# Letting the first two FFN blocks start on half a block of tokens, in a fused top-k attention and SwiGLU kernel

## The chip, the cores and the metric

The kernel runs on one core of one Trainium2 chip. The metric is device time in microseconds of one execution. A core has a TensorE (PE, with its weight loads listed apart as PEld), a VectorE (DVE), a ScalarE (ACT), a GpSimd (POOL) and DMA queues. Each engine works through its own instructions in the order in which the program emitted them and waits for the others by semaphores, so where in the program a piece of work is emitted decides what stands behind it.

## What is computed

```python
# attention: batch 8, heads 8, seq 576, head_dim 64, float32
scores = scale * np.matmul(q, k.transpose(0, 1, 3, 2))
kth = np.partition(scores, -32, axis=-1)[..., -32:-31]
scores = np.where(scores >= kth, scores, -1e9)
attn = softmax(scores)                       # abridged
attn_out = np.matmul(attn, v)
# bridge: (B,H,S,D) -> x of (4608 tokens, 512)
g = x @ w_gate                               # 512 -> 1536
silu = g * (1.0 / (1.0 + np.exp(-g)))
val = x @ w_val                              # 512 -> 1536
out = silu * val @ w_out                     # 1536 -> 512
```

## The kernel before

**Units and turns.** Attention is cut into 160 units, in the order batch, query tile, head pair. A batch has four query tiles of 128 tokens and a fifth of 64, each with four head pairs; a unit of a full tile handles two heads side by side, one of the fifth tile handles its two heads of 64 rows in one go, so it is half a unit of VectorE work. The main loop makes one *turn* for each unit. In turn `n`, VectorE selects the 32 largest scores of unit `n`; ScalarE and GpSimd weigh unit `n-1`; TensorE transposes the weights of unit `n-3`, multiplies those of unit `n-4` by the values, and computes the scores of unit `n+1`.

**FFN pieces.** What attention leaves goes to `xT`, in 18 blocks of 256 tokens. When a block has all its tokens from all head pairs (`done`), its FFN is fed to TensorE in *pieces*: 24 pieces of gate and value products (four matmuls of 256 columns each) and 12 pieces of the output product. A turn adds 4.6 (a half unit's turn 2.3) to a credit that is capped at 8, and a piece costs 1.

**Rounding of the weights.** The three weight matrices arrive in 72 pieces of 128 x 256, and each goes through ScalarE, GpSimd and VectorE before it may be used. This is spread over the turns: in five of every eleven VectorE steps a `rounding(1)` is made, which emits one stage of each of several pieces.

```python
    def weights():
        # ... 48 pieces of w_gate and w_val in turns, then 24 of w_out
        lags = (5, 3, 2, 0)
        for n in range(len(pieces) + lags[0]):
            for lag in lags:
                if 0 <= n - lag < len(pieces):
                    next(pieces[n - lag], None)
            ready[0] = max(n - lags[0] + 1, 0)
            yield

    def rounded(src, dst):                      # four stages, cut
        nc.sync.dma_start(w[:], ...);                                   yield
        nc.scalar.activation(size[:], high.bitcast(FP32), AF.Abs)       # L101
        nc.gpsimd.tensor_scalar(size[:], size[:], HUGE, LEAST, ...)     # L103
        nc.scalar.mul(ulps[:], low.bitcast(U32), 2.0**-29);             yield   # L106
        nc.vector.tensor_scalar(bits, bits, 3, 0x3FFFFFFF, ...)         # L110
        nc.gpsimd.tensor_tensor(bits, bits, ulps[:], ALU.add);          yield   # L113
        nc.vector.scalar_tensor_tensor(out=dst.bitcast(I32), ...)       # L116

    def need(n):
        while ready[0] < n:
            next(weight)
# ...
    def feed(kb):                               # the FFN of one block
        x = xT.pop(kb)
        hs = []
        def product(w, s, then):
            ps = ps_f.tile([P, 2, BLK], FP32, tag="f", name="f")
            need(8 * s + (4 if w is wg else 8))
            for i in range(2):
                m = 2 * s + i
                for kc in range(KC):            # 4
                    nc.tensor.matmul(ps[:, i, :], w[:, kc, m * P : (m + 1) * P],
                                     x[:, kc, :], ...)                  # L412
                if i == 1:
                    on_act.append(lambda: then(ps))
                yield
        for s in range(MS):                     # 6
            h = ffn.tile([P, 2, BLK], FP32, tag="h", name="h", bufs=MS + 1)
            hs.append(h)
            def gate(ps, h=h):
                nc.scalar.activation(h[:], ps[:], AF.Tanh, scale=0.5)   # L430
                nc.scalar.mul(half[:], ps[:], 0.5)                      # L431
                nc.scalar.add(h[:], h[:], 1.0)                          # L432
                on_pool.append(lambda: nc.gpsimd.tensor_mul(h[:], h[:], half[:]))  # L433
            def value(ps, h=h):
                nc.scalar.copy(val[:], ps[:])                           # L437
                on_pool.append(lambda: nc.gpsimd.tensor_mul(h[:], h[:], val[:]))   # L438
            yield from product(wg, s, gate)
            yield from product(wv, s, value)
        for t in range(BLK // P):
            for m in range(MC):                 # 12
                need(8 * MS + 2 * m + 2)
                nc.tensor.matmul(ps[:], hs[m // 2][:, m % 2, t * P : (t + 1) * P],
                                 wo[:, m, :], ...)                      # L449
                # ... evacuation and store after the last
                if m % 2 == 1:
                    yield

    def piece():
        # ... flush what waits for ScalarE and GpSimd, if there is more than one
        while True:
            if not current:
                if not todo or done.get(todo[0], 0) < NHP * BLK:
                    return False
                current.append(feed(todo.pop(0)))
            if next(current[0], 0) == 0:
                current.pop()
                continue
            return True
    def pieces(n):
        for _ in range(n):
            if credit[0] >= 1 and piece():
                credit[0] -= 1
# ...
    for n in range(NU + VALUES):                # one turn
        if n >= NU - NHP: credit[0] = 8.0
        else: credit[0] = min(credit[0] + (4.6 if nh == 2 else 2.3), 8.0)
        flush(on_act)
        # ... penalize(n-1): POOL e L293
        flush(on_pool)
        # ... turn(n-3): PE etps L329; finish_unit(n-4): PE av L349, L358
        # ... scores(n+1): PE s L250; weigh(n-1): ACT e L302; ACT sc L255
        dve(2, beside=False)
        pieces(2)
        flush(on_act); flush(on_pool)
        dve(1); dve(1)
        # ... normalize(n-2), part of prep
        pieces(1); dve(1); pieces(1); dve(2)
        run(topk)                               # ends with DVE e L281
        pieces(6)
    while piece():
        pass
```

Of the kernel before, what the change touches and what calls it, by code (L numbers as in the profile page):

```python
# [8 lines left out]
AF = mybir.ActivationFunctionType  # L9
ALU = mybir.AluOpType  # L10
FP32 = mybir.dt.float32
# [4 lines left out]
P = 128  # L16
# [4 lines left out]
BLK = 256  # L21
# [6 lines left out]
def kernel(  # L28
# [27 lines left out]
    nc = tc.nc  # L56
# [5 lines left out]
    NHP = H // 2  # L62
    KC = DM // P
    MC = DFF // P
    MS = MC // 2
    NBLK = B * S // BLK
    scale = 1.0 / float(D) ** 0.5
# [8 lines left out]
    ffn = ctx.enter_context(tc.tile_pool(name="ffn", bufs=2))  # L76
# [11 lines left out]
    wg = consts.tile([P, KC, DFF], FP32, name="wg")  # L88
    wv = consts.tile([P, KC, DFF], FP32, name="wv")
# [31 lines left out]
    def weights():  # L121

        pieces = []
        for f in range(0, DFF, WP):
            for src, dst in ((w_gate, wg), (w_val, wv)):
                for c in range(KC):
                    pieces.append((src[c * P : (c + 1) * P, f : f + WP], dst[:, c, f : f + WP]))
        for c in range(MC):
            for f in range(0, DM, WP):
                pieces.append((w_out[c * P : (c + 1) * P, f : f + WP], wo[:, c, f : f + WP]))  # L130
        pieces = [rounded(*p) for p in pieces]
# [8 lines that stand above are left out]
    ready = [0]  # L140
    weight = weights()
# [2 lines left out]
        for _ in range(n):  # L144
            next(weight, None)

    def need(n):

        while ready[0] < n:
            next(weight)  # L150

    pairs = [(b, hp) for b in range(B) for hp in range(NHP)]
    raw, preps = {}, {}
# [184 lines left out]
    xT, done = {}, {}  # L338
# [41 lines left out]
    def store(o, g0):  # L380

        at = g0
        while at < g0 + P:
            b, c = divmod(at, S)
            j, p0 = divmod(c, P)
            n = min(g0 + P - at, S - c, P - p0)
            r0 = b * S + (c if j == J else J * p0 + j)
            dst = out[r0 : r0 + n, :] if j == J else out[r0 : r0 + J * (n - 1) + 1 : J, :]
            nc.sync.dma_start(dst, o[at - g0 : at - g0 + n, :])
            at += n  # L390

    on_act, on_pool = [], []

    def flush(queue):
        while queue:
            queue.pop(0)()

    def feed(kb):

        x = xT.pop(kb)
        hs = []

        def product(w, s, then):
            ps = ps_f.tile([P, 2, BLK], FP32, tag="f", name="f")
            need(8 * s + (4 if w is wg else 8))
            for i in range(2):
                m = 2 * s + i  # L410
                for kc in range(KC):
                    nc.tensor.matmul(  # L412
                        ps[:, i, :],
                        w[:, kc, m * P : (m + 1) * P],
                        x[:, kc, :],
                        start=(kc == 0),
                        stop=(kc == KC - 1),
                    )
                if i == 1:
                    on_act.append(lambda: then(ps))  # L420
                yield

        for s in range(MS):
            h = ffn.tile([P, 2, BLK], FP32, tag="h", name="h", bufs=MS + 1)
            hs.append(h)


            def gate(ps, h=h):
                half = ffn.tile([P, 2, BLK], FP32, tag="gv", name="half_g", bufs=3)
                nc.scalar.activation(h[:], ps[:], AF.Tanh, scale=0.5)  # L430
                nc.scalar.mul(half[:], ps[:], 0.5)  # L431
                nc.scalar.add(h[:], h[:], 1.0)  # L432
                on_pool.append(lambda: nc.gpsimd.tensor_mul(h[:], h[:], half[:]))  # L433

            def value(ps, h=h):
                val = ffn.tile([P, 2, BLK], FP32, tag="gv", name="val", bufs=3)
                nc.scalar.copy(val[:], ps[:])  # L437
                on_pool.append(lambda: nc.gpsimd.tensor_mul(h[:], h[:], val[:]))  # L438

            yield from product(wg, s, gate)  # L440
            yield from product(wv, s, value)
        for t in range(BLK // P):
            ps = ps_f.tile([P, DM], FP32, tag="f", name="o_ps")
            for m in range(MC):
                need(8 * MS + 2 * m + 2)
                if m == 6:
                    flush(on_act)
                    flush(on_pool)
                nc.tensor.matmul(  # L449
                    ps[:],  # L450
                    hs[m // 2][:, m % 2, t * P : (t + 1) * P],
                    wo[:, m, :],
                    start=(m == 0),
                    stop=(m == MC - 1),
                )
                if m == MC - 1:

                    def finish(ps=ps, t=t):
                        o = ffn.tile([P, DM], FP32, tag="o", name="o")
                        nc.scalar.copy(o[:], ps[:])  # L460
                        store(o, kb * BLK + t * P)

                    on_act.append(finish)
                if m % 2 == 1:
                    yield

    NU = len(units)
    todo = list(range(NBLK))
    current = []

    def piece():

        if len(on_act) > 1:
            flush(on_act)
        if len(on_pool) > 1:
            flush(on_pool)
        while True:
            if not current:
                if not todo or done.get(todo[0], 0) < NHP * BLK:
                    return False  # L480
                flush(on_act)
                flush(on_pool)
                current.append(feed(todo.pop(0)))
            if next(current[0], 0) == 0:
                current.pop()
                continue
            return True

    def fetch(n):

# [5 lines left out]
            load(i + NHP)  # L496

    def pieces(n):
        for _ in range(n):
            if credit[0] >= 1 and piece():  # L500
                credit[0] -= 1

    def run(steps):
        for _ in steps:
# [14 lines left out]
    credit = [0.0]  # L519
# [4 lines left out]
    for n in range(NU + VALUES):  # L524
# [37 lines left out]
        if n < NHP:  # L562
            load_v(n)
# [3 lines that stand above are left out]
# [12 lines left out]
    while piece():  # L579
        pass  # L580
# [48 lines left out]
```

## Time and profile before

| What | Value |
|---|---|
| time, median of three runs | 1914.77 us (1911.7 to 1914.82) |
| span of the profiled execution | 1913.4 us |
| busy: PE, DVE, ACT, POOL | 1756.5, 1608.9, 1156.3, 816.0 us |
| gate and value matmuls (L412), records of 256 columns | 3456, in 1728 of each weight |
| output matmuls (L449), records of 512 columns | 864 |
| first gate product starts at | 167.1 us |
| last selection on VectorE ends at | about 1820 us |

Shares of busy time are averages over stages with different limits, so the span is best cut at the turns. The last VectorE instruction of a turn's selection is `e L281`, so its starts date the ends of the turns. A float32 matmul of this kernel appears in the trace as two MATMUL records, each with a weight load of its own, while a transpose appears as one. The duration of a MATMUL record contains the time in the pipeline; what a row of matmuls takes is seen from the distance of their starts. In the timeline a group of like instructions is one row: start, length from the first start to the last end, engine, line, shapes and number.

### The profile page before, as it was taken

What the parts mean: (1) busy time and instruction counts of PE and PEld (TensorE: products, weight loads), DVE (VectorE), ACT (ScalarE), POOL (GpSimd) and SP (SyncE); (2) the same over time, 40 slices, a digit from 0 to 9 for tenths busy, and PEclk for the clock granted to TensorE, in tenths of its full rate; (3) what the DMA queues carried; (4) which work ended last, traced back from release to release, by engine and by line L of the source; (5) the groups of instructions that cost most, each with busy time, mean ns of one, the idle gap of its engine ahead of it and who ended that gap; (6) DMA issues with size and microseconds to landing.
All of it is one profiled execution on the core that took longest, in us unless ns stands there. A gap on an engine that the chain in (4) does not pass through costs nothing.

```text
span 1913.4 us, 29363 instructions
## 1 busy us (share of the span) xinstructions
PE 1756.5 (92%) x10144; PEld 1297.0 (68%) x10144; DVE 1608.9 (84%) x3476; ACT 1156.3 (60%) x2821; POOL 816.0 (43%) x846
## 2 busy tenths in 40 slices
PE   3437789989999999999999999999999999999999
PEld 2336558667677777676768676868686868586866
DVE  7999889998899979998799979999799989999400
ACT  5656656566666656675657566656675656665421
POOL 4566644335343525353335343525243535353412
PEclk7668899989999999999999999999999999999999
DMA  7322202000300012000210003000210001000000
GB/s 185 88 78 82 67 22 69 11 1 3 76 12 12 2 27 63 12 1 13 53 37 1 12 4 87 1 12 1 60 31 12 1 14 45 18 1 12 1 12 11
DMA packets 111253, 59.58 MB, mean 31 GB/s; under 512 B 89088, under 2 KB 97280, under 8 KB 111104
## 3 DMA queue, kind: packets, MB, share of 16 engines
q1 hardware_dynamic: 109904, 57.41, 11.5%
q8 instruction: 80, 1.31, 0.3%
q14 instruction: 69, 0.57, 0.1%
q10 hardware_dynamic: 1200, 0.30, 0.1%
HBM read 48.23 MB, written 9.44 MB: 30 GB/s over the span
## 4 chain that ended last, share of the span: by engine, by line
PE 82%; DVE 6%; POOL 5%; ACT 4%; issue 2%; DMA 0%; SPq 0%; POOLq 0%; DVEq 0%; ACTq 0%
PE f L412 38%; PE o_ps L449 19%; PE av L358 8%; PE etps L329 7%; PE s L250 7%; DVE m L271 2%; POOL e L293 2%; DVE rest L275 2%; PE s L236 2%; ACT e L302 1%; PE av L349 1%; PE kqps L205 1%; ACT sc L255 1%; POOL size L113 1%; POOL size L103 1%
## 5 line engine op out<-in xcount | busy, mean ns | idle before, releaser
L271 DVE MAX8 m<-rest 128x8 f32<-128x576 f32 x864 | 615.2, 747 | 2.2
L275 DVE MATCH_REPLACE8 rest<-m,rest 128x576 f32<-128x576 f32 x576 | 424.1, 743 | 0.0
L412 PE MATMUL f<-xT,wg 128*128 128x256 f32 x1728 | 407.5, 386 | 0.0
L293 POOL TENSOR_TENSOR e<-e,sc 128x1152 f32<-128x1152 f32 (+1 forms) x160 | 382.7, 2392 | 42.4 <-DVE e L281 38.8
L412 PE MATMUL f<-xT,wv 128*128 128x256 f32 x1728 | 395.8, 381 | 0.0
L449 PE MATMUL o_ps<-wo,h 128*128 128x512 f32 x864 | 387.6, 598 | 0.0
L412 PEld LDWEIGHTS f<-xT,wg 128*128 128x128 f32 x1728 | 324.2, 191 | 71.5 <-issue 29.9
L412 PEld LDWEIGHTS f<-xT,wv 128*128 128x128 f32 x1728 | 325.3, 190 | 53.3 <-issue 10.5
L433 POOL TENSOR_TENSOR h<-h,half_g 128x512 f32<-128x512 f32 x108 | 138.4, 1282 | 453.0 <-ACT h L432 435.0
L271 DVE MAX8 m<-sc 128x8 f32<-128x576 f32 x288 | 205.6, 750 | 123.9 <-ACT sc L255 78.8
L329 PE MATMUL etps<-ident,e 128*128 128x128 f32 (+1 forms) x1312 | 187.5, 288 | 125.9 <-POOL size L103 48.1
L449 PEld LDWEIGHTS o_ps<-wo,h 128*128 128x128 f32 x864 | 159.4, 190 | 193.1 <-issue 186.9
L329 PEld LDWEIGHTS etps<-ident,e 128*128 128x128 f32 (+1 forms) x1312 | 159.4, 147 | 176.1 <-POOL size L103 51.3
L330 ACT COPY et<-etps 128x512 f32<-128x512 f32 (+1 forms) x448 | 184.7, 482 | 148.5 <-PE etps L329 147.1
L302 ACT ACTIVATE e<-e,bias 128x576 f32<-128x576 f32 x288 | 222.1, 776 | 74.9 <-POOL e L293 74.5
L317 ACT ACTIVATE e<-e,tot 128x576 f32<-128x576 f32 x288 | 210.5, 780 | 5.4 <-DVE tot L314 5.1
L275 DVE MATCH_REPLACE8 rest<-m,sc 128x576 f32<-128x576 f32 x288 | 211.9, 742 | 0.0
L438 POOL TENSOR_TENSOR h<-h,val 128x512 f32<-128x512 f32 x108 | 139.7, 1293 | 149.6 <-ACT val L437 149.6
L250 PE MATMUL s<-kqT 64*128 64x288 f32 x1024 | 173.1, 446 | 9.6 <-ACT kqT L210 6.4
L312 POOL TENSOR_SCALAR tot<-tot 128x2 f32<-128x2 f32 (+1 forms) x160 | 37.4, 234 | 329.3 <-ACT e L302 320.9
L358 PE MATMUL av<-et,v 128*64 128x128 f32 (+1 forms) x2560 | 174.6, 282 | 0.0
L255 ACT COPY sc<-s 128x288 f32<-128x288 f32 x512 | 165.0, 410 | 2.5 <-PE s L250 2.5
(44 smaller groups left out, 1436.0 us busy)
## 6 DMA issues: line engine op xcount, KB each, us to landing
kq_in<-in_k_dram SPq DMA_DIRECT2D x64, 128.0 KB, 2.8
v<-in_v_dram SPq DMA_DIRECT2D x32, 256.0 KB, 3.0
kq_in<-in_q_dram SPq DMA_DIRECT2D x62, 128.0 KB, 3.1
w<-in_moe_w_gate_dram SPq DMA_DIRECT2D x24, 256.0 KB, 2.7
w<-in_moe_w_val_dram SPq DMA_DIRECT2D x24, 256.0 KB, 2.7
w<-in_moe_w_out_dram SPq DMA_DIRECT2D x24, 256.0 KB, 2.6
out_dram<-o SPq DMA_DIRECT2D x40, 128.0 KB, 2.4
out_dram<-o SPq DMA_DIRECT2D x16, 256.0 KB, 2.3
```

Of the source, the lines that this page charges most:

```text
L250: nc.tensor.matmul(ps[:, 0:half], slab[d, q0 : q0 + P], slab[d, k0 : k0 + half])
L255: nc.scalar.copy(sc[:, i * half : (i + 1) * half], ps[:, 0:half])
L271: nc.vector.max(m[:, t, 8 * r : 8 * r + 8], cur[:, hs])
L275: nc.vector.match_replace(rest[:, hs], m[:, t, 8 * r : 8 * r + 8], cur[:, hs], LOWEST)
L293: nc.gpsimd.tensor_tensor(e[:, every], e[:, every], sc[:, every], ALU.add)
L302: nc.scalar.activation(e[:, hs], e[:, hs], AF.Exp, bias=bias[:, t : t + 1], scale=scale, accum_out=tot[:, t : t + 1],)
L317: nc.scalar.mul(e[:, hs], e[:, hs], tot[:, t : t + 1])
L329: nc.tensor.transpose(ps[0:kl, c * P : (c + 1) * P], e[:, k0 : k0 + kl], ident[:])
L330: nc.scalar.copy(et[0:kl, c0 : c0 + cn, :], ps[0:kl, 0 : cn * P].rearrange("p (c j) -> p c j", c=cn),)
L358: nc.tensor.matmul(av[hh * R : (hh + 1) * R, 0:ql], v_last[:, hh, :] if c == J else vt[:, hh, c, :], moving, start=last and c == 0, stop=c ...
L412: nc.tensor.matmul(ps[:, i, :], w[:, kc, m * P : (m + 1) * P], x[:, kc, :], start=(kc == 0), stop=(kc == KC - 1),)
L449: nc.tensor.matmul(ps[:], hs[m // 2][:, m % 2, t * P : (t + 1) * P], wo[:, m, :], start=(m == 0), stop=(m == MC - 1),)
```

## The change

The gate and value products of blocks 0 and 1 are made in two halves of 128 columns. A half may start when its own 128 tokens are there, which for block 0 is four units earlier than the whole block. Where the weights for a product aren't rounded yet, the FFN no longer forces the rounding (`need`), but gives up its place in this turn (`until` yields 0) and tries again at the next. A piece of a half costs half a credit. The output product and the other 16 blocks stay as they were, and so does everything in attention.

```diff
-    def need(n):
+    def until(n):
         while ready[0] < n:
-            next(weight)
+            yield 0
...
+    def parts(kb):
+        return [slice(0, P), slice(P, BLK)] if kb < 2 else [slice(0, BLK)]
...
-        def product(w, s, then):
+        def product(w, s, c, then):
+            n = c.stop - c.start
+            yield from until(8 * s + (4 if w is wg else 8))
             ps = ps_f.tile([P, 2, BLK], FP32, tag="f", name="f")
-            need(8 * s + (4 if w is wg else 8))
             for i in range(2):
                 m = 2 * s + i
                 for kc in range(KC):
                     nc.tensor.matmul(
-                        ps[:, i, :],
+                        ps[:, i, 0:n],
                         w[:, kc, m * P : (m + 1) * P],
-                        x[:, kc, :],
+                        x[:, kc, c],
...
-                    on_act.append(lambda: then(ps))
-                yield
+                    on_act.append(lambda: then(ps[:, :, 0:n], c))
+                yield n / BLK
...
+        for c in parts(kb):
+            while done[kb] < NHP * c.stop:
+                yield 0
+            for s in range(MS):
+                if c.start == 0:
+                    hs.append(ffn.tile([P, 2, BLK], FP32, tag="h", name="h", bufs=MS + 1))
+                h = hs[s]
...             # gate and value as before, on the columns c of h, half_g and val
...
-                need(8 * MS + 2 * m + 2)
+                yield from until(8 * MS + 2 * m + 2)
...
                 if m % 2 == 1:
-                    yield
+                    yield 1
...
-                if not todo or done.get(todo[0], 0) < NHP * BLK:
-                    return False
+                if not todo or done.get(todo[0], 0) < NHP * parts(todo[0])[0].stop:
+                    return 0
...
     def pieces(n):
-        for _ in range(n):
-            if credit[0] >= 1 and piece():
-                credit[0] -= 1
+        while n > 0 and credit[0] >= 1:
+            size = piece()
+            if not size:
+                break
+            n -= size
+            credit[0] -= size
```

More of the change, by code (lines that the diff above doesn't have):

```diff
@@ L396, in flush @@
             queue.pop(0)()
+    def parts(kb):
+        return [slice(0, P), slice(P, BLK)] if kb < 2 else [slice(0, BLK)]
     def feed(kb):
-        x = xT.pop(kb)
+        x = xT[kb]
         hs = []
-        def product(w, s, then):
+        def product(w, s, c, then):
+            n = c.stop - c.start
+            yield from until(8 * s + (4 if w is wg else 8))
             ps = ps_f.tile([P, 2, BLK], FP32, tag="f", name="f")
-            need(8 * s + (4 if w is wg else 8))
             for i in range(2):
@@ L419, in product, with gate, value @@
                 if i == 1:
-                    on_act.append(lambda: then(ps))
-                yield
[L423 to L441, printed above, removed]
+                    on_act.append(lambda: then(ps[:, :, 0:n], c))
[7 more added lines that the diff above has]
+                h = hs[s]
+                def gate(ps, c, h=h):
+                    half = ffn.tile([P, 2, BLK], FP32, tag="gv", name="half_g", bufs=3)
+                    hc, gc = h[:, :, c], half[:, :, c]
+                    nc.scalar.activation(hc, ps, AF.Tanh, scale=0.5)
+                    nc.scalar.mul(gc, ps, 0.5)
+                    nc.scalar.add(hc, hc, 1.0)
+                    on_pool.append(lambda: nc.gpsimd.tensor_mul(hc, hc, gc))
+                def value(ps, c, h=h):
+                    val = ffn.tile([P, 2, BLK], FP32, tag="gv", name="val", bufs=3)
+                    hc, vc = h[:, :, c], val[:, :, c]
+                    nc.scalar.copy(vc, ps)
+                    on_pool.append(lambda: nc.gpsimd.tensor_mul(hc, hc, vc))
+                yield from product(wg, s, c, gate)
+                yield from product(wv, s, c, value)
+        del xT[kb]
         for t in range(BLK // P):
@@ L483, in piece @@
                 current.append(feed(todo.pop(0)))
[L484 to L487, printed above, removed]
+            size = next(current[0], None)
+            if size is not None:
+                return size
+            current.pop()
     def fetch(n):
```

## The prediction, made before the changed kernel was run

> **What bounds the kernel now.** I read first the busy shares in 40 slices of the span, then the sums by stage, then the dates of the turns.
>
> ```profile
> PE   3437789989999999999999999999999999999999
> ...
> DVE  7999889998899979998799979999799989999400
> ...
> PEclk7668899989999999999999999999999999999999
> ```
>
> TensorE is idle for a good half of the first three slices (of 47.8 us) and full from the eighth on. The change aims at this hole. I cut the span where the FFN starts (turn 11), where the rounding of the weights ends (turn 15), and where block 1 is finished (turn 27). In the view of windows each row has the stretch, its length, and the busy time of PE, PEld, DVE, ACT and POOL, then the granted clock:
>
> ```profile
> 110.00:166.00 56.00, 23.18 (x142) 18.76 (x141) 52.95 (x130) 35.02 (x93) 33.25 (x49) 0.63 0.29 86
> 166.00:253.00 87.00, 74.38 (x383) 57.18 (x383) 71.95 (x160) 54.28 (x134) 55.23 (x71) 0.92 0.18 56
> 253.00:372.00 119.00, 114.34 (x676) 81.20 (x675) 109.97 (x234) 74.28 (x184) 48.77 (x49) 0.99 0.15 38
> 372.00:405.00 33.00, 24.85 (x143) 16.90 (x143) 31.51 (x70) 20.53 (x52) 9.33 (x10) 0.83 0.02 9
> 405.00:1800.00 1395.00, 1371.37 (x8105) 1018.45 (x8102) 1239.19 (x2642) 877.65 (x2128) 586.46 (x555) 1.00 0.09 21
> ```
>
> To 166 VectorE is the bound (53 of 56). From 166 to 253 no engine is (PE 74, DVE 72 of 87). From 253 to 372 it is TensorE (114 of 119), with VectorE close. From 372 to 405 TensorE waits again: block 2 has no tokens yet. After 405 TensorE is the bound to the end.
>
> The dates of the turns, from the timeline of VectorE (the last operation of a selection, for turns 6, 10, 15, 25, 27 and 30; two records in a full turn, one in a half):
>
> ```profile
> 108.89 1.18 DVE L281 TENSOR_SCALAR e<-sc,m 128x576 f32<-128x576 f32 x2
> ...
> 165.71 1.42 DVE L281 TENSOR_SCALAR e<-sc,m 128x576 f32<-128x576 f32 x2
> ...
> 252.41 0.93 DVE L281 TENSOR_SCALAR e<-sc,m 128x576 f32<-128x576 f32 x2
> ...
> 346.56 1.19 DVE L281 TENSOR_SCALAR e<-sc,m 128x576 f32<-128x576 f32 x2
> ...
> 371.16 0.93 DVE L281 TENSOR_SCALAR e<-sc,m 128x576 f32<-128x576 f32 x2
> ...
> 404.43 0.94 DVE L281 TENSOR_SCALAR e<-sc,m 128x576 f32<-128x576 f32 x2
> ```
>
> A turn with rounding and no FFN takes 56.8 / 4 = 14.2 us (turns 7 to 10). One with both takes 86.7 / 5 = 17.34 us (turns 11 to 15), so the FFN adds 3.1 us to each, 15.7 in all, though neither PE nor DVE is full. Why is seen on VectorE in turn 12:
>
> ```profile
> 192.52 0.41 DVE L116 SCALAR_TENSOR_TENSOR wo<-w,size 128x256 int32<-128x256 int32 x1
> 195.81 0.29 DVE L110 TENSOR_SCALAR size<-size 128x256 int32<-128x256 int32 x1 [2.88 <-POOL size L103]
> ```
>
> VectorE waits 2.88 us for a rounding step on GpSimd (L103), which stands behind the step on ScalarE (L101), and that one behind the three gate operations of the FFN, made from 191.64 to 193.12; on GpSimd the gate's multiply of 1.27 us (L433) lies between as well.
>
> **What the Trainium skill says.** The page "TensorE: Matmul & The Clock Gate", section "Back-to-back issue gap", gives N / 2.4 ns plus 2.5 between matmuls of N columns, so half the columns take half the time; its section "LDWEIGHTS (loading the stationary operand)" puts a load at columns / 1.2, which is 107 ns for 128. The trace of before has both: nine transposes, each a load of 128 columns and a matmul of 128, go by in 0.98 us (602.43 to 603.41), 109 ns each; eight gate records of 256 columns take 1.73 us, 216 ns each. A half record should thus cost 109 ns, with its load just hidden. The same page, section "What's actually happening", has the clock at half after an idle window of about 3.4 us; the trace agrees, as the nine transposes take 1.95 us after each idle gap of 8 us. "VectorE: DVE Perf Modes", section "The TRN2 errata — SBUF-src ops pay a fixed extra latency per instruction", says that small ScalarE operations don't shrink with their size. The trace agrees: 512 columns take 597 ns, 256 take 444 (L430, L101).
>
> **The change part by part.** The order of emission doesn't depend on time, so I followed credit, `done` and `ready` turn by turn through the program's own rules. Before: no product ever finds its weights unrounded, so `need` forces nothing. FFN credits spent in turns 11 to 27 are 8, 4, 5, 4, 5 (two of them output) | 2, 2, 3, 2 | 5, 4, 5, 4, 5, 5, 4, 5: 72 for two blocks. None is spent in turns 28 to 30, and the credit stands at 8 when block 2 comes in turn 31.
>
> After, in turns 7 to 27: 7.5, 1.5, 2, 1 | 7.5, 4.5, 3, 1, 1 | 7.5, 2, 2.5, 2 | 4.5, 5, 4.5, 5, 4, 5, 1, 0: again 72. The first half of block 0 runs in turns 7 to 10, held back by the rounding from turn 8 on. The second runs in turns 11 and 12, since its tokens come at turn 11 as before; the output product then crawls in turns 13 to 15, as `wo` isn't rounded. Its remaining seven pieces come in a heap in turn 16, a half turn, followed at once by block 1.
>
> In turn 31 both programs are in the same state, and from there they emit the same instructions in the same order. TensorE is idle in turns 28 to 30 in both, so nothing carries over: the whole effect is by how much turn 30 ends earlier or later than 404.4. The 12 credits that move ahead of turn 11 fill idle TensorE time, but shorten the path only where TensorE is the bound.
>
> *Turns 7 to 15.* Bare: 9 x 14.2 = 127.8 us, before 143.5 with 15.7 of surcharge. The surcharge comes from ScalarE and GpSimd operations that stand ahead of the rounding. For a gate of 512 columns these are 1.48 + 1.27 = 2.75 us; of 256, three starts 0.33 us apart (the distance of L101 and L106 at 256 columns) and a multiply of 0.74 (L113): 1.73, so 63%. There are 24 halves in place of 12 wholes: 15.7 x 2 x 0.63 = 19.8. I take off 2 for turns 9 and 10, whose few products fit into slack. So 18, or **+2 us**.
>
> *Turns 16 to 27.* Turn 16 gets 7.5 credits where it had 2. A credit is 1.73 us, so 9.5 us more on TensorE; of this 3.3 fall into the idle time before turn 17's transposes (259.12), some 3 more into idle time and a cold clock of turns 17 and 18 that the heap removes, and 0.9 are given back in turn 18 (2.5 for 3). That leaves about 2 us of lateness. Turns 19 to 25 have 30 credits in both, so it stays. Turns 26 and 27 lose 8 credits, but VectorE has 10.56 us in each (its pace in turn 28), and before they took 24.6: the most to be had is 3.5, and most of it isn't, as their lateness is that of scores made behind turn 25's pieces, which stay. A cold TensorE at turn 16, after three nearly empty turns, costs another 1. So **+2 us**, if the matmuls of halves run at 109 ns.
>
> Sum: +4, less 1 for a warmer TensorE in turns 8 to 16, so 1914.8 + 3 = 1918.
>
> **The rivals.** (a) *The hole gets filled:* the FFN of half a block vanishes into idle time and the surcharge isn't paid in turns 7 to 10, because TensorE was idle 60% there. Then the surcharge is only that of the 12 half products in turns 11 and 12 (10 us for 15.7), and turns 26 and 27 give their 3.5: about 1906. For it speaks the idle TensorE, against it that VectorE was busy 53 of 56 us there and that the rounding waits for ScalarE and GpSimd, not for TensorE. The floor, with no surcharge at all (-15.7) and turns 16 to 27 at VectorE's pace (8 x 10.56 + 4 x 5.28 = 105.6 us for 118.8, so -13), is 1886. (b) *Loads bind the halves:* a gate load has a record of 190 ns where a transpose's has 148; if a half record took 150 ns in place of 109, block 1's 384 half records, in turns where TensorE is the bound, would cost 384 x 0.041 = 16 us: 1934. Against it: the loads of av (L358, 64 columns, no transposes) follow each other at 64 ns (16 from 615.96 to 616.98), about 128 for 128 columns. (c) *Heaps:* 7.5 credits (13 us) in turn 7 hold up ScalarE, then the rounding in turn 8, more than I took; with the heap in turn 16 this could make 10 us more: 1928.
>
> **Range and chances.** I predict 1918 us. Rival (a) sets the low end at 1906, (b) and (c) the high end at 1930. A change of 2% is 38 us, more than the floor of (a) gains and about what (b) and (c) at their worst cost together. Faster by over 2%: 0.01; within: 0.97; slower: 0.02.
>
> **What would show it.** The first gate product starts near 109 us (turn 7) rather than 167. Turn 15 ends near 254, where it ended at 252.4; earlier than 247 speaks for (a). Half records start 109 ns apart; 150 would be (b). In turns 8 and 12 VectorE waits for L103 as before. Turn 16's TensorE work is some 17 us long and turn 17 starts late. From turn 31 on all rows are the same, shifted by one number. I am wrong if that later part changes by itself, or if turns 7 to 10 keep their 14.2 us with the FFN in them.

## The result, and the profile after

The changed kernel takes 1921.74 us (median of 6 runs, 1921.6 to 1922.17) against 1914.12 us before (6 runs, 1911.7 to 1914.82). The ratio is 1.0042, 95% interval 1.0029 to 1.0055: 7.6 us slower, inside the range and within 2%, on the side that was forecast and some 4 us beyond the 1918 that was.

The busy shares in 40 slices of the changed kernel:

```profile
PE   3466789869999999999899999999999999999999
...
DVE  7988889998899979998799979999799989999400
...
PEclk7688899989999999999999999999999999999989
```

TensorE has its first FFN work in the third slice (at 109.8 us) where before it came in the fourth (167.1). The third slice rises from 3 to 6 tenths for it, and the fourth, eighth and ninth fall by 1, 1 and 2: work has moved forward, and the span hasn't got shorter. The dates of the turns in the timeline of VectorE (ends of turns 6, 10, 15, 19, 25 and 30):

```profile
108.36 1.18 DVE L281 TENSOR_SCALAR e<-sc,m 128x576 f32<-128x576 f32 x2
...
175.51 1.42 DVE L281 TENSOR_SCALAR e<-sc,m 128x576 f32<-128x576 f32 x2
...
254.04 0.94 DVE L281 TENSOR_SCALAR e<-sc,m 128x576 f32<-128x576 f32 x2
...
288.63 0.52 DVE L281 TENSOR_SCALAR e<-sc,m 128x576 f32<-128x576 f32 x1
...
358.00 0.94 DVE L281 TENSOR_SCALAR e<-sc,m 128x576 f32<-128x576 f32 x2
...
412.31 0.95 DVE L281 TENSOR_SCALAR e<-sc,m 128x576 f32<-128x576 f32 x2
```

Differences of such dates are the yardstick for all that follows. Turns 7 to 15 take 145.7 us (143.5 before), turns 16 to 19 34.6 (27.3), turns 20 to 25 69.4 (66.9), turns 26 to 30 54.3 (57.9). So +2.2, +7.3, +2.5 and -3.6: turn 30 ends 8 us later than before. What follows it is the same program in both. Busy times in the stretches between those dates, from the view of windows of the changed kernel (stretch, length, PE, PEld, DVE, ACT, POOL, then the granted clock):

```profile
108.40:175.50 67.10, 44.19 (x308) 38.05 (x305) 58.02 (x131) 41.72 (x114) 42.19 (x61) 0.83 0.24 74
175.50:254.00 78.50, 58.03 (x395) 43.36 (x395) 68.35 (x159) 49.32 (x133) 51.88 (x73) 0.87 0.20 62
254.00:288.60 34.60, 34.08 (x238) 24.48 (x238) 25.22 (x51) 18.93 (x49) 11.03 (x14) 0.98 0.07 21
288.60:358.00 69.40, 68.67 (x580) 56.77 (x577) 64.04 (x137) 46.27 (x134) 32.12 (x39) 1.00 0.23 56
358.00:412.30 54.30, 34.28 (x215) 23.72 (x215) 52.86 (x116) 33.16 (x83) 16.18 (x17) 0.87 0.02 6
```

The third row is where most of the time went: in turns 16 to 19 TensorE is busy for 34.1 of 34.6 us and VectorE for 25.2. The last row is where some came back: VectorE is busy 52.9 of 54.3.

What happens there starts with the heap of turn 16. On VectorE, the end of turn 17 and the first operation of turn 18:

```profile
267.58 0.52 DVE L281 TENSOR_SCALAR e<-sc,m 128x576 f32<-128x576 f32 x1
274.41 0.76 DVE L271 MAX8 m<-sc 128x8 f32<-128x576 f32 x1 [6.31 <-ACT sc L241]
```

Turns 16 and 17 still run on scores made earlier (7.3 and 6.25 us); turn 18 waits 6.31 us for its scores to be copied by ScalarE (L241). ScalarE in the same time:

```profile
269.56 0.58 ACT L472 COPY o<-o_ps 128x512 f32<-128x512 f32 x1 [7.75 <-PE o_ps L461]
270.88 1.24 ACT L330 COPY et<-etps 128x512 f32<-128x512 f32 x3 [0.74 <-PE etps L329]
...
273.62 0.69 ACT L241 COPY sc<-s 128x288 f32<-128x288 f32 x2
```

And TensorE:

```profile
258.09 11.43 PE L461 MATMUL o_ps<-wo,h 128*128 128x512 f32 x26 [0.23 <-DVE wo L116]
269.36 1.05 PE L417 MATMUL f<-xT,wg 128*128 128x128 f32 x8
270.25 1.15 PE L329 MATMUL etps<-ident,e 128*128 128x128 f32 x9
...
272.57 1.19 PE L236 MATMUL s<-kqT 64*64 64x288 f32 x8
```

TensorE makes the heap of output records for 11.4 us. The scores of unit 18 stand behind it and start at 272.57. ScalarE's 7.75 us of idle time before the copy of the block's output are an effect of the heap and not what holds up the scores: TensorE works without a gap from 258.09 to 277.53, and ScalarE is idle again (0.74 us) before the next copies. In the kernel before, the same scores started 9.9 us earlier:

```profile
262.64 1.81 PE L236 MATMUL s<-kqT 64*64 64x288 f32 x8
```

VectorE didn't wait for them there. A half turn has only 6.25 us of VectorE work to cover a delay, so in the changed kernel VectorE waits 6.31 us.

### The profile page after: what moved, and what is told of

Same layout as the page of the kernel before. It is cut to its first block, busy times and chain, and to the rows that moved or that the text cites. A ratio compares the mean times of both kernels' runs of the same rounds, so it can differ in the third digit from the quotient of the medians.

```text
span 1920.2 us, 30215 instructions
## 1 busy us (share of the span) xinstructions
PE 1757.8 (92%) x10528; PEld 1308.7 (68%) x10528; DVE 1611.0 (84%) x3476; ACT 1159.8 (60%) x2869; POOL 820.1 (43%) x870
## 3 DMA queue, kind: packets, MB, share of 16 engines
q8 instruction: 83, 1.36, 0.3%
## 4 chain that ended last, share of the span: by engine, by line
PE 80%; DVE 7%; POOL 5%; ACT 4%; issue 3%; DMA 0%; SPq 0%; POOLq 0%; DVEq 0%; ACTq 0%
PE f L417 38%; PE o_ps L461 18%; PE av L358 7%; PE etps L329 7%; PE s L250 6%; DVE m L271 3%; DVE rest L275 3%; POOL e L293 2%; PE s L236 2%; PE av L349 1%; ACT e L302 1%; PE kqps L205 1%; ACT sc L255 1%; POOL size L113 1%; POOL size L103 1%
## 5 line engine op out<-in xcount | busy, mean ns | idle before, releaser
L417 PE MATMUL f<-xT,wv 128*128 128x256 f32 (+1 forms) x1920 | 406.0, 363 | 17.5 <-DVE wv L116 9.5
L417 PE MATMUL f<-xT,wg 128*128 128x256 f32 (+1 forms) x1920 | 411.8, 365 | 4.5 <-DVE wg L116 4.5
L461 PE MATMUL o_ps<-wo,h 128*128 128x512 f32 x864 | 392.9, 604 | 16.5 <-DVE wo L116 16.5
L293 POOL TENSOR_TENSOR e<-e,sc 128x1152 f32<-128x1152 f32 (+1 forms) x160 | 382.9, 2393 | 49.0 <-DVE e L281 33.4
L417 PEld LDWEIGHTS f<-xT,wv 128*128 128x128 f32 x1920 | 338.2, 193 | 69.9 <-issue 12.2
L417 PEld LDWEIGHTS f<-xT,wg 128*128 128x128 f32 x1920 | 335.0, 192 | 70.3 <-issue 28.1
L443 POOL TENSOR_TENSOR h<-h,half_g 128x512 f32<-128x512 f32 (+1 forms) x120 | 141.6, 1180 | 450.5 <-ACT h L442 433.7
L329 PEld LDWEIGHTS etps<-ident,e 128*128 128x128 f32 (+1 forms) x1312 | 159.9, 147 | 143.9 <-issue 66.9
L449 POOL TENSOR_TENSOR h<-h,val 128x512 f32<-128x512 f32 (+1 forms) x120 | 141.4, 1178 | 164.5 <-ACT val L448 164.0
L250 PE MATMUL s<-kqT 64*128 64x288 f32 x1024 | 168.9, 440 | 9.0 <-ACT kqT L210 5.8
L358 PE MATMUL av<-et,v 128*64 128x128 f32 (+1 forms) x2560 | 168.5, 276 | 0.0
L440 ACT ACTIVATE h<-f 128x512 f32<-128x512 f32 (+1 forms) x120 | 66.8, 557 | 165.0 <-PE f L417 163.6
```

Source lines behind the costliest of these rows:

```text
L250: nc.tensor.matmul(ps[:, 0:half], slab[d, q0 : q0 + P], slab[d, k0 : k0 + half])
L293: nc.gpsimd.tensor_tensor(e[:, every], e[:, every], sc[:, every], ALU.add)
L329: nc.tensor.transpose(ps[0:kl, c * P : (c + 1) * P], e[:, k0 : k0 + kl], ident[:])
L358: nc.tensor.matmul(av[hh * R : (hh + 1) * R, 0:ql], v_last[:, hh, :] if c == J else vt[:, hh, c, :], moving, start=last and c == 0, stop=c ...
L417: nc.tensor.matmul(ps[:, i, 0:n], w[:, kc, m * P : (m + 1) * P], x[:, kc, c], start=(kc == 0), stop=(kc == KC - 1),)
L443: on_pool.append(lambda: nc.gpsimd.tensor_mul(hc, hc, gc))
```

## The experiments

Each is compared with the kernel before, run beside it on the same chip. The ratio is worked out from all executions of both, not from the medians. The table gives the turns' times in us from the timeline of VectorE, one profiled execution each; "t7-15" is from the end of turn 6 to the end of turn 15. The profiled execution of e1_late took 4.7 us more than the median of its kernel, that of e4_even_before 3.5 us less; the others lie within 1 us.

| Kernel | t7-15 | t16-19 | t20-25 | t26-30 | median, us | ratio (interval) |
|---|---|---|---|---|---|---|
| before | 143.5 | 27.3 | 66.9 | 57.9 | 1914.1 | |
| the change | 145.7 | 34.6 | 69.4 | 54.3 | 1921.7 | 1.0042 (1.0029, 1.0055) |
| e1_late | 147.5 | 28.1 | 70.1 | 55.8 | 1917.6 | 1.0027 (1.0017, 1.0038) |
| e2_spread16 | 146.0 | 26.0 | 68.8 | 55.8 | 1914.5 | 1.0010 (1.0001, 1.0018) |
| e3_even_after | 146.4 | 26.0 | 63.0 | 52.8 | 1907.8 | 0.9968 (0.9957, 0.9980) |
| e4_even_before | 142.4 | 28.6 | 64.5 | 52.8 | 1910.9 | 0.9984 (0.9977, 0.9992) |
| e5_lag_before | 133.9 | 27.4 | 66.9 | 57.9 | 1900.3 | 0.9928 (0.9914, 0.9941) |
| e6_lag_even_after | 135.7 | 26.3 | 64.0 | 52.8 | 1892.5 | 0.9886 (0.9873, 0.9900) |
| e7_forced | 153.9 | 28.2 | 67.6 | 53.6 | 1923.4 | 1.0048 (1.0034, 1.0061) |
| e8_lag_even_before | 130.9 | 29.3 | 64.5 | 52.8 | 1895.7 | 0.9905 (0.9892, 0.9919) |
| e9_lag_after | 137.0 | 36.5 | 69.4 | 54.3 | 1912.0 | 0.9989 (0.9983, 0.9996) |
| e10_even_before_31 | 130.7 | 29.3 | 64.5 | 52.8 | 1894.0 | 0.9897 (0.9880, 0.9913) |
| e11_even_after_again | 135.7 | 26.3 | 64.0 | 52.8 | 1892.1 | 0.9882 (0.9867, 0.9897) |

**The halves without the early start (e1_late).**

```diff
-                if not todo or done.get(todo[0], 0) < NHP * parts(todo[0])[0].stop:
+                if not todo or done.get(todo[0], 0) < NHP * BLK:
```

> The change, but a block starts only when all its 256 tokens are there, as before; its products are still made in halves of 128 columns. Credits in turns 11 to 27 are then as before (7.5, 4.5, 4.5, 4.5, 5 ...), with no heap in turns 7 and 16. Theory A (the 7.6 us come from heaps and from pieces emitted just in time, mostly at turn 16): only the doubled ScalarE and GpSimd operations are left, my 15.7 to 19.8 us in turns 11 to 15, so 1914 + 1 to 4 = 1915 to 1918, and turns 16 to 30 last 152 us as before. Rival B (the halves themselves cost it, by their width and their number of instructions): 1920 to 1922, with turns 20 to 25 longer than their 66.9 us before.

1917.6 us, 3.6 more than before by the medians and 5 by the ratio. Turns 7 to 15 took 3.95 us longer, as expected. This isolates the term that I had worked out for the doubled ScalarE and GpSimd operations: with 127.8 us bare, the surcharge is 147.5 - 127.8 = 19.7 us, for 19.8 estimated. But turns 16 to 30 took 154.1 us, not the 152 of theory A: turns 20 to 25 got 3.3 us longer (70.1 for 66.9), which only rival B expected, and turns 26 to 30 gave 2 back. So the halves aren't free, in the rounding turns above all. The median lies in theory A's range, the profiled execution (1922.4 us) just above rival B's, so that the turns of this one trace may show more than the kernel usually loses. Whether the halves make the loss of the change is for the next run to tell.

**The heap of turn 16 spread over turns 16 to 27 (e2_spread16).**

```diff
-            credit[0] = min(credit[0] + (4.6 if nh == 2 else 2.3), 8.0)
+            credit[0] = min(credit[0] + (4.6 if nh == 2 else 2.3), 3.0 if 16 <= n < 20 else 8.0)
```

> The change, with the credit capped at 3 in turns 16 to 19, so that the heap of 7.5 credits in turn 16 becomes 3, 2, 2, 2 and the rest moves to turns 20 to 27. Theory A: the 7.3 us that turns 16 to 19 took more than before (34.6 for 27.3) go to 1 or 2; some comes back as lateness in turns 26 and 27, which get 5 and 1 credits in place of 1 and 0. 1915 to 1918. Rival B (halves): nothing changes, 1920 to 1922. Rival C (TensorE simply has its sum of work in turns 16 to 27, wherever it lies): nothing changes either, but turns 26 and 27 then take what turns 16 to 19 give.

Turns 16 to 19 fall from 34.6 to 26.0 us, and turns 20 to 30 give back only 0.9 (124.6 for 123.7). 1914.5 us: by the ratios 6 and by the medians 7 of the 7.6 us are gone, with the same halves and the same early start. The same dates in the timeline of VectorE (ends of turns 17, 18 and 19):

```profile
267.98 0.52 DVE L281 TENSOR_SCALAR e<-sc,m 128x576 f32<-128x576 f32 x1
274.22 0.52 DVE L281 TENSOR_SCALAR e<-sc,m 128x576 f32<-128x576 f32 x1
280.47 0.52 DVE L281 TENSOR_SCALAR e<-sc,m 128x576 f32<-128x576 f32 x1
```

The three half turns run at VectorE's 6.25 us without a gap. TensorE still waits for `wo` to be rounded in turns 13 to 16, as in the change (17.3 us in all between 200 and 256 us, 16.3 in the change), so that wait alone isn't what cost the time: it was the heap. The two runs without a heap in turn 16 for other reasons (e1_late and e7_forced) have 28.1 and 28.2 us there. Rival C falls, since the same work a few turns later doesn't take the time with it.

**Even spreads, with and without the early start (e3_even_after, e4_even_before).** The rate and the cap make the credits of blocks 0 and 1 come out by turn 30.

```diff
+        elif n < 31:
+            credit[0] = min(credit[0] + (3.6 if nh == 2 else 1.8), 4.0)    # with the change
+            credit[0] = min(credit[0] + (4.0 if nh == 2 else 2.0), 4.0)    # with the kernel before
         else:
             credit[0] = min(credit[0] + (4.6 if nh == 2 else 2.3), 8.0)
```

> The change, with 3.6 credits per full turn and a cap of 4 up to turn 30, so that the 72 credits of blocks 0 and 1 are spread over turns 7 to 29 at 3.5 a turn (2 in the half turns), and turn 31 starts in the same state as ever. Theory A: no heap, so turns 16 to 30 go to VectorE's pace of 10.56 us (5.3 to 6.2 in the half turns), 140 to 146 us for 158 now; turns 7 to 15 keep 143 to 147. Total 1902 to 1910, faster than both. Rival B (halves cost): 1916 or more. Rival D (turns 7 to 30 are bound by the sum of surcharges, spread or not): 1914 to 1922.

> The kernel before, with 4.0 credits per full turn and a cap of 4 up to turn 30: 4 a turn from turn 11 to turn 30, no early start, no halves. Theory A: turns 20 to 27, where before TensorE was the bound with 4 to 5 credits, go to VectorE's pace; 3 to 6 us gained, and 2 more in turns 11 and 12 without the heap of 8: 1906 to 1911. If this is as fast as the even spread with the change, the early start itself is worth nothing and only the heaps mattered; if the change with the even spread is faster by 3 us or more, the early start is worth that. Rival D: 1914 as before.

1907.8 us with the change and 1910.9 without, both in the ranges of theory A. With the change, turns 16 to 30 fall to 141.8 us; VectorE then does its 10.56 us in each full turn from 21 to 30, so the halves cost nothing there when they come at 3.5 credits a turn. The kernel before gains as well, 152.0 to 146.0. The medians are 3 us apart, which I had named as the sign that the early start is worth that much; but turn 30 ends only 0.7 us earlier with it (396.5 for 397.2), and the two don't emit the same program from turn 31 on, as the last pair below shows. Turns 7 to 15 aren't touched (146.4 and 142.4): spread or in heaps, early or late, they carry about the same surcharge. There rival D is right, and that asks for its cause.

**Slack for the rounding (e5_lag_before, e6_lag_even_after).** One step more between the stage on ScalarE and GpSimd and the one on VectorE:

```diff
-        lags = (5, 3, 2, 0)
+        lags = (6, 4, 2, 0)
-        w = ffn.tile([P, n, 2], I32, tag="w", name="w", bufs=6)
+        w = ffn.tile([P, n, 2], I32, tag="w", name="w", bufs=7)
...     # size: bufs 4 to 5; o: bufs 2 to 1; ulps overwrites `low` in place of its own tile
```

> The kernel before, with one rounding step more between the stage on ScalarE and GpSimd (L101, L103, L106) and the stage on VectorE (L110): lags (6, 4, 2, 0) for (5, 3, 2, 0). To make room, the ulps are written over the low words that they come from, and the output tile has one buffer; nothing else moves, and the FFN credits of the turns are the same. Theory E (the surcharge of the FFN in turns with rounding is VectorE waiting at L110 for an L103 that stands one step behind it and has FFN operations ahead of it; such waits sum to 18.1 us in turns 7 to 15): they nearly vanish, turns 7 to 15 take 127 to 133 us for 143.5, total 1900 to 1906. Rival F (ScalarE and GpSimd or the memory ports are bound by their sum of work there): 140 us or more, 1911 to 1915.

> The change with the even spread (3.6 credits, cap 4 up to turn 30) and with that longer lag of the rounding. Theory E: turns 7 to 15 take 127 to 134 us for 146.4, turns 16 to 30 stay at 141 to 143 us; total 1892 to 1898, below both kernels and below the even spread alone (1907.8). Rival F: 1905 to 1909.

1900.3 and 1892.5 us, both in the ranges of theory E. Turns 7 to 15, with 133.9 and 135.7 us, were 0.9 and 1.7 us above theirs; a gain of 5 us before turn 7, which I hadn't counted, made up for it. VectorE's waits in turns 7 to 15 of the kernel before (total in us, number, longest):

```profile
DVE size L110 <- POOL size L103: 18.1, 9, 3.5
```

and in the same turns with the longer lag:

```profile
DVE wo L116 <- POOL size L113: 3.7, 4, 1.1
DVE size L110 <- POOL size L103: 1.5, 5, 0.3
```

Of 18.1 us of waits 5.2 are left, and turns 7 to 15 are 9.6 us shorter. The difference went into VectorE's own operations, which are busy 3.4 us longer there (128.8 for 125.4): five L110 now run beside L113 on GpSimd and take 0.83 us each in place of 0.29. Turns before 7, which have no FFN, gained as well: turn 6 ends at 103.7 in place of 108.9, and 10.4 us of waits for L103 there are gone.

So the tight hand-over costs time with or without the FFN. Of the 9.6 us, 3.0 lie in turns 7 to 10, which have no FFN in this kernel. In turns 11 to 15 the surcharge over such turns, now 13.46 us each, is still 80.1 - 67.3 = 12.8 us, where it was 15.7. Theory E was right about the waits, but these are not the whole surcharge: 5.1 us of what is left are waits, and 7.6 are VectorE's longer operations, L110 and L116 foremost. They are the subject of the last section.

The operations themselves kept their lengths (L106 447 ns for 441, L113 755 for 741), so nothing shows that the room made for the longer lag helped by itself; the extra buffers weren't run without the lag. The two mends, longer lag and even spread, nearly add up: 14.1 us (1914.4 to 1900.3) and 6.1 (1914.0 to 1907.8, with the change) alone, 21.9 together (1914.4 to 1892.5).

**Forcing the rounding (e7_forced).**

```diff
     def until(n):
         while ready[0] < n:
-            yield 0
+            next(weight)
+        yield from ()
```

> The change, but a product whose weights aren't rounded forces their rounding, as the kernel before would have (its own early start never came about, so it forced nothing). Halves of block 0 then take 7.5 and 4.5 credits in turns 7 and 8, 7.5 and 4.5 in turns 11 and 12; turn 8 rounds 14 steps in place of 4 or 5, and turn 15 has the last. The output product of block 0 no longer crawls (5, 4, 3 in turns 13 to 15), so there is no heap in turn 16 (2.5). Theory A: the heap of turn 16 is gone (7 us back), while turn 8 gets some 10 to 15 us longer and turns 9 to 14 give about as much back; 1913 to 1919. If forced rounding is by itself the harm that the change means to avoid: above 1922.

1923.4 us, 4 above the upper end of theory A and in the range that I had named for forced rounding as a harm by itself. Against the change that isn't clear of noise: the intervals overlap (1.0034 to 1.0061 and 1.0029 to 1.0055). The heap of turn 16 is gone (28.2 us), as foreseen. But turn 8, with its 14 rounding steps, takes 37.4 us, 18 more than in the change, and turns 9 to 15 give back only some 10 of them. Neither that forcing is a harm by itself nor that passing over is a gain is shown: forced, the block pays in the rounding turns what it saves later.

**The longer lag with the change as it is (e9_lag_after), and both mends without the change (e8_lag_even_before, e10_even_before_31).**

> The change as it is, with the longer lag of the rounding alone. Theory A + E: the heap of turn 16 stays (turns 16 to 19 take some 34 us), the waits for L103 in turns 7 to 15 go: 1905 to 1910, so 5 to 9 us slower than the kernel before with the same lag (1900.3), as the change was without it. If the loss of the change were mostly in the rounding turns, it would come within 3 us of 1900.3.

1912.0 us, 2 above what I expected, with a wide spread (1908.8 to 1914.6). The heap stays, and is worse: 36.5 us in turns 16 to 19, while turns 7 to 15 are 8.7 us shorter than in the change. The change costs more with the slack than without it: the ratios 0.9989 and 0.9928 are some 12 us apart, for 7.6 without slack and 5 to 9 expected.

> The kernel before with both mends and no early start: 4.0 credits with a cap of 4 up to turn 30, and the longer lag of the rounding. If the two mends add up (lag -14, even spread -3 to -6): 1894 to 1898. If the early start of the change is worth something once there is no heap and the rounding has slack, this is slower than the change with both mends (1892.5) by 2 to 5 us; if the early start is worth nothing, both are within 1.5 us.

1895.7 us by the clock, but turn 30 ended at 380.7, 2 us *before* that of the change with both mends (382.6). The credit left at turn 31 differed between the two (0.6 and 0 after turn 31, with 4 and 8 pieces in it), so they weren't the same program afterwards. Hence a direct pair, with the credit set to 8 in turn 31 of the one, and e6 once more as the other:

```diff
+        elif n == 31:
+            credit[0] = 8.0
```

> The kernel before with both mends (4.0 credits, cap 4, up to turn 30; longer lag), and the credit set to 8 in turn 31, so that from turn 31 on it emits just what the change with both mends emits. The early start is then the only thing that differs, with the halves that it needs. If the early start is worth something with heaps and tight rounding gone: 2 to 4 us slower than e11. If not: within 1.5 us, as turn 30 ended at 380.7 us without it and at 382.7 with it in the two traces so far.

> The change with both mends once more, unaltered (e6), on the same chip and in the same call as e10, so that the two are compared directly: 1890 to 1895.

1894.0 without the early start and its halves, 1892.1 with them. That is between the two expectations; the intervals (0.9880 to 0.9913 and 0.9867 to 0.9897) overlap, and turn 30 ends 1 us later *with* it (382.5 for 381.5). In the traces the lead comes only after turn 30, where both emit the same instructions: 1412.6 us with the early start and 1415.4 without, up to the end of turn 159. One and the same kernel, e6 and e11, differs there as much (1415.0 and 1412.6). So what the early start is worth once heaps and tight rounding are gone stays open: 2 us by the clock, -1 by the end of turn 30. The fastest version, 1892.1 to 1892.5 us, beats both kernels by 1.1% or more, and nearly all of it comes from the two mends.

## Why the prediction was right, and where it was not

**The schedule.** That the two programs differ only in turns 7 to 30 held. From the end of turn 30 to that of turn 159, before takes 1415.4 us and after 1412.8. The 2.6 us between them need no cause in the change, since two executions of one kernel (e6 and e11) differ by 2.4 there.

**Turns 7 to 15.** I said +2, made of 15.7 us of surcharge becoming 18. Measured: 145.7 - 127.8 = 17.9. The parts weren't all as I put them: turn 9 (14.3 us) had slack for its products as I took it, turn 10 (16.5) had not; turns 13 to 15 came in 0.8 under their bare 42.6. The mechanism, ScalarE and GpSimd operations of the FFN ahead of the rounding, is shown for VectorE's waits by two runs: with the operations doubled in e1_late the waits for L103 go from 18.1 to 23.1 us, and with a step of slack in e5_lag_before to 1.5. But waits are not the whole surcharge. Of the 2.2 us that the change added, 1.1 are waits (19.2 for 18.1) and 1.0 is VectorE busy longer with the same operations (126.4 for 125.4), for which my sum had no term; of the 15.7 us before, 11.2 were waits above those of turns 7 to 10 and 4.5 longer operations. That the sum came out to 0.1 us in both kernels is thus in part luck.

**Rival (a), the hole that gets filled,** is refuted: turns 7 to 10 took 67.2 us for 56.8, with 12 credits in them. TensorE being idle there was no room for work, since each piece brings ScalarE and GpSimd work too, and these two had the rounding: VectorE waited 9.1 us for L103 where it had waited 3.1, and was busy 4.3 us longer.

**Rival (b), loads that bind the halves.** In turn 7 of the changed kernel (TensorE's timeline):

```profile
109.76 2.05 PE L417 MATMUL f<-xT,wg 128*128 128x128 f32 x16
111.65 1.95 PE L417 MATMUL f<-xT,wv 128*128 128x128 f32 x16
113.44 1.95 PE L417 MATMUL f<-xT,wg 128*128 128x128 f32 x16
```

16 half records from 111.65 to 113.44 make 112 ns each, not 150: half of this case's 216 ns, to 4 ns. My reading of the Trainium skill was wrong, though. The formula of "Back-to-back issue gap" (page "TensorE: Matmul & The Clock Gate"), given there for single matmuls apart from a stream, makes 109 ns of 256 columns and 56 of 128; the records of this float32 kernel are spaced twice as far, so the trace of before did not have both, as I wrote. The 109 ns stand on the trace's own figures alone, its transposes and half of 216. The 3 ns above 109 come to 384 x 0.003 = 1.2 us for block 1, a part of the 3.3 us that e1_late showed in turns 20 to 25. The rest of these I can't place; VectorE waited 6.6 us there for 3.8 before, and with 3.5 credits a turn (e3_even_after) it doesn't wait for scores there.

**Turns 16 to 27.** This is the step that was mis-sized. I wrote "+2 us" with "about 2 us of lateness" left of the heap. Up to turn 30 it was 158.3 - 152.0 = +6.3. The mechanism was right, the heap of turn 16 delays what comes after; the term of the sum that failed is "some 3 more into idle time and a cold clock of turns 17 and 18". I followed TensorE, where turn 17's transposes indeed came 16.8 us after turn 16's, as I had said ("some 17"), and let the idle time of turn 18 take up a part of that. But the scores of unit 18, which VectorE needs next, stand ahead of that idle time. They started 9.9 us later than before (272.57 for 262.64). Of these, 5.0 were there before the heap: turn 16's transposes began later, behind a piece of turn 15 that had waited 3.9 us for `wo`. In the changed kernel, and below it in the kernel before:

```profile
251.59 2.08 PE L461 MATMUL o_ps<-wo,h 128*128 128x512 f32 x2 [3.90 <-DVE wo L116]
253.45 2.05 PE L329 MATMUL etps<-ident,e 128*128 128x128 f32 x9
...
248.44 1.39 PE L329 MATMUL etps<-ident,e 128*128 128x128 f32 x9 [0.68 <-POOL size L113]
```

The heap made it 6.1 more up to turn 17's transposes (my 9.5 less the idle 3.3), and only 1.2 came back from there to the scores. Nor did I ask how much VectorE work a half turn has to bridge such a gap: 6.25 us, where a full turn has 10.56. VectorE waited 6.31 us, and turns 16 to 19 cost +7.3.

In the other direction, I wrote of the 3.5 us of turns 26 and 27 that "most of it isn't" to be had; 2.0 were (22.6 for 24.6), and turn 29 gave 1.6 more that I hadn't looked for. VectorE's waits for scores in turns 26 to 30 went from 4.5 to 1.4 us with next to no FFN left in them. Rival (c) named the heap of turn 16 rightly; but of the 10 us that it put on the heaps of turns 7 and 16 together, some 5 came in turns 16 to 19 and none in turns 7 to 15, which took what I had said.

**Smaller slips of the working.** A half turn is 6.25 us of VectorE, not the 5.28 of the floor in rival (a), which rises from 1886 to some 1890 us. 2% is 38 us, and (b) and (c) at their worst come to 16 + 10 = 26; (b) alone, at 1934, lies outside the range that it was to set.

**A warmer TensorE,** for which I took off 1 us, is there in the records (turn 8's nine transposes take 0.98 us, 131.54 to 132.52, for 1.95 before), but turn 8 was the longest of turns 7 to 10 all the same (19.05 us); no gain from it is to be seen.

## What to carry to other kernels

Idle time on one engine is not room for work, if each piece of that work has to pass through other engines' queues, where it will stand ahead of somebody's critical step: look at what the engine's partners have in the same turns. An early start moves little if what comes back later is emitted in a heap: spread it. By the account above a heap does most harm where the bound engine has the least work to bridge it (here a half turn of 6 us); a heap in a full turn wasn't compared with it. And before moving work around a tight hand-over between engines, give the hand-over a step of slack: here that was worth 14 us, twice the damage of the change, and a good half of it in turns without any FFN.

## What the runs showed of the hardware that was not expected

VectorE's last rounding step (L116), with two tensor inputs, takes 0.41 us. When it starts while GpSimd runs its two-input add of 2.6 us (L293), it ends 0.28 us after that add, in all six such cases of the two kernels. In turn 8 of the changed kernel, on VectorE:

```profile
131.14 2.68 DVE L116 SCALAR_TENSOR_TENSOR wg<-w,size 128x256 int32<-128x256 int32 x1
```

and on GpSimd:

```profile
130.90 2.65 POOL L293 TENSOR_TENSOR e<-e,sc 128x1152 f32<-128x1152 f32 x1
```

The step before it (L110), with one tensor input, can be held in the same way. In turn 12 of the kernel before it took 1.36 us in place of 0.29, beside a two-input multiply of the FFN:

```profile
189.12 1.36 DVE L110 TENSOR_SCALAR size<-size 128x256 int32<-128x256 int32 x1
188.88 1.45 POOL L438 TENSOR_TENSOR h<-h,val 128x512 f32<-128x512 f32 x1
```

The Trainium skill, page "VectorE: DVE Perf Modes", section "Two Vector instructions with no wait between them", has the second input of a VectorE operation read through an interface that VectorE shares with GpSimd, and the only input too where the operation runs in a mode that uses two ports. The records fit it; in which mode L110 ran, no run here shows. Two hits on L116 fall into turns 7 to 10 of the changed kernel (2.68 and 1.81 us, so some 3.7 lost) and none into those turns before, where the one hit of this size (2.44 us) comes in turn 12. L116 takes 11.6 us in all in these turns of the changed kernel and 7.8 before, which is most of the 4.3 us by which VectorE is busy longer there. I had not counted this; no experiment here isolates it.
